# Attention and channel mix on one core: q and k transposed in fp32 as loaded, cast to bf16 in the copy out of PSUM

## The chip, the cores and the metric

The kernel runs on one core of one Trainium2 chip. The metric is the time of one execution on the device, in microseconds (us). Ratios come with a 95% interval. The kernel before took 274.27 us (median of 2 runs, 273.6 to 274.94).

Some names. TensorE (PE in the profile) does matrix products and transposes and writes to PSUM. VectorE is DVE, ScalarE is ACT, GpSimd is POOL, and SyncE (SP) issues most DMAs. A *pair* is two heads of one batch: there are 8 batches of 4 pairs, so pairs 0 to 31. Times inside an execution are counted from the start of its span.

## The reference

```python
# q, k, v: (8, 8, 576, 64) fp32; d_model = 512, d_ff = 1024
scores = q @ k.transpose(0, 1, 3, 2) / sqrt(64)          # per head, 576 x 576
scores = where((rel >= 0) & (rel < 128), scores - slope[h] * abs(rel), -1e9)
attn = softmax(scores); x = attn @ v                     # heads side by side: (8, 576, 512)
x_prev = x shifted by one position
xk = mu_k * x + (1 - mu_k) * x_prev;  xr = likewise with mu_r
out = sigmoid(xr @ w_r) * (relu(xk @ w_k) ** 2 @ w_v)
```

The scores need q and k with the head dimension on the partitions, so both are transposed on the chip. The products of the second half are the greater part of TensorE's work.

## The kernel before

For each pair, q and k are loaded in fp32, cast to bf16, transposed by TensorE eight blocks at a time into one PSUM bank, and copied out by ScalarE into `qk_buf`. The listing is shortened: `...` stands for what is left out.

```python
# H = 8, D = 64, G = 4 pairs per batch, NF = 4, NBUF = 4, SM = 512 rows (the other 64 go another way)
p_sa = pool(bufs=2, PSUM)   # scores: 2 banks each
p_tp = pool(bufs=1, PSUM)   # transposes: one bank
p_mm = pool(bufs=3, PSUM)   # matmuls: one bank each; all 8 banks are taken
ldr = cst.tile([128, 2, NBUF, 2, NF * D], FP32, name="ldr")      # q|k, slot, head, 4 rows of 64

def load_qk(it, npair=1, part=None):
    ...
        if part is None:                                         # 1 KB runs
            nc.sync.dma_start(out=dst, in_=hs[:, 0:SM].rearrange("h (p r) d -> p h (r d)", p=128))
    ...
def pool_cast(dst, src):
    nc.gpsimd.tensor_scalar(out=dst, in0=src, scalar1=1.0, scalar2=0.0, op0=ALU.mult, op1=ALU.add)
def vec_cast(dst, src):
    nc.vector.tensor_copy(out=dst, in_=src)

def cast_qk(it, part=None, fq=pool_cast, fk=vec_cast):
    ...                                                          # r0, r1: rows 0 to NF where part is None
    cs = csp.tile([128, 2, NF, 2, D], BF16, tag="cs", name="cs", bufs=4)
    T["cs", it, part] = cs
    for i, f in ((0, fq), (1, fk)):
        f(cs[:, i, 0:r1 - r0].rearrange("p r h d -> p h r d"),   # puts the two heads side by side
          ldr[:, i, it % NBUF].rearrange("p h (r d) -> p h r d", d=D)[:, :, r0:r1])

def transp(it):
    ...
    cs = T.pop(("cs", it, None))
    tp = p_tp.tile([128, 1024], BF16, tag="tp", name="tp")
    for n in range(2 * NF):
        nc.tensor.transpose(tp[:, 128 * n:128 * n + 128],
                            cs[:, n // NF, n % NF].rearrange("p h d -> p (h d)"), ident)
    nc.scalar.copy(out=qk_buf[it % NBUF].rearrange("p t (c r) -> p t c r", r=NF),
                   in_=tp.rearrange("p (t r c) -> p t c r", t=2, r=NF))

def scores(it, pieces, m0):
    ...                                                          # matmuls of qk_buf into sa
    nc.scalar.activation(out=ah, in_=sa[:, :, 0:w], func=AF.Exp, scale=float(scale))
    if not early:                                                # batches 2 to 7: the mask multiply
        nc.vector.tensor_tensor(out=ah, in0=ah, in1=mask[...], op=ALU.mult)

def feed(it, fk=vec_cast):
    cast_qk(it, None, pool_cast, fk)
    cast_v(it)                                                   # GpSimd
    load_qk(it + 4)
    load_v(it + 4)
    ...
```

Batch 0 has its own path and does not change. Batch 1 (pairs 4 to 7) runs while weights and inputs still load. From pair 8 a loop puts work on TensorE pair by pair, with matmuls of the second half (`run_units`) between the steps. In this loop the program fixes the order of TensorE, SyncE and GpSimd; a scheduler orders VectorE and ScalarE.

```python
    for it in range(2 * G, NIT + 2):
        scores_full(it)
        ...                               # bud: how much of the second half goes into this pair
        run_units(bud * .3)
        av(it - 1, 0, NJ)                 # attention times v
        run_units(bud * .3)
        ...                               # in one pair of four, the tails
        transp(it + 2)
        feed(it + 3)
        ...
        run_units(bud * .4)
        outT(it - 1, 0, NJ)               # transposes of the result, also through p_tp
```

The softmax here doesn't subtract the row's maximum and nothing guards it: scores larger than these inputs give would overflow.

## Time and profile before

| | kernel before |
|---|---|
| time, median of 2 | 274.27 us |
| span of the profiled execution | 272.5 us |
| start of pair 8's scores / from pair 8 to pair 31 / rest | 70.8 / 162.5 / 39.2 us |

The three stages are read from the starts of the score matmuls in the trace. The first block is part of the profile's page: busy time by engine, and the chain of work that ended last, by engine.

```profile
## 1 busy us (share of the span) xinstructions
PE 244.9 (90%) x2272; PEld 145.0 (53%) x2304; DVE 211.4 (78%) x428; ACT 179.9 (66%) x293; POOL 74.0 (27%) x121
...
q1 hardware_dynamic: 71040, 37.76, 51.8%
...
PE 54%; DVE 15%; ACT 11%; DMA 8%; SPq 5%; issue 5%; POOL 2%; DVEq 0%; POOLq 0%; ACTq 0%
```

TensorE is busy 90% of the span and holds 54% of the chain, so it bounds most of the kernel, with VectorE (78%) behind it. The line of q1 is the main DMA queue: packets, MB, and the share of the 16 DMA engines' time.

The next block has groups of instructions of the same kernel, with shapes kept apart: line, engine, operation, output from inputs, count, then busy time and the mean in ns, then idle time of the engine just before.

```profile
L235 DVE TENSOR_TENSOR at<-at,mask 128x1024 bf16<-128x1024 bf16 x48 | 44.6, 968 | 0.8 <-ACT at L233 0.8
L187 ACT COPY qk<-tp 128x1024 bf16<-128x1024 bf16 x28 | 28.4, 1016 | 10.9 <-PE tp L184 10.6
L126 POOL TENSOR_SCALAR cs<-ldr 128x512 bf16<-128x512 f32 x34 | 27.7, 815 | 7.7 <-DMA ldr<-in_q_dram 6.7 <-DMA ldr<-in_k_dram 0.4
L184 PE MATMUL tp<-ident,cs 128*128 128x128 bf16 x224 | 17.1, 219 | 0.0
L184 PEld LDWEIGHTS <-cs 128*128 128x128 bf16 x224 | 14.3, 98 | 4.8 <-issue 0.6 <-POOL cs L126 0.2
L130 DVE CAST cs<-ldr 128x512 bf16<-128x512 f32 x22 | 9.8, 443 | 4.4 <-DMA ldr<-in_k_dram 4.4
```

The casts are L126 on GpSimd (34, among them k's where GpSimd casts both) and L130 on VectorE (22). A bf16 transpose is recorded with 219 ns, but the records of consecutive transposes overlap, so this is not the time that one takes up on TensorE. That time is read from the timeline of TensorE (start, length, engine, line, count), here around one pair's transposes:

```profile
151.18 0.61 PE L184 MATMUL tp<-ident,cs 128*128 128x128 bf16 x8
151.62 1.03 PE L341 MATMUL pv<-wv_sb,kk 128*128 128x512 bf16 x4
```

Eight transposes occupy TensorE for 151.62 - 151.18 = 0.44 us, about 55 ns each.

Last, the table of windows over a steady stretch (after the window: busy us of each engine and number of its instructions, granted TensorE clock, share of the DMA engines, GB/s), and the timeline of VectorE in two places, with GpSimd's between them. All are of the kernel before.

```profile
core 0: us, PE busy (x) PEld busy (x) DVE busy (x) ACT busy (x) POOL busy (x), PEclk, DMA share, GB/s
105.00:164.00 59.00, 56.44 (x553) 33.75 (x558) 54.23 (x102) 42.82 (x66) 17.52 (x20) 1.00 0.59 161
```

```profile
112.52 2.12 DVE L235 TENSOR_TENSOR at<-at,mask 128x1024 bf16<-128x1024 bf16 x2
...
112.33 0.76 POOL L126 TENSOR_SCALAR vs<-vdr 128x512 bf16<-128x512 f32 x1 [3.25 <-issue]
113.06 1.04 POOL L126 TENSOR_SCALAR cs<-ldr 128x512 bf16<-128x512 f32 x1
...
229.91 1.28 DVE L235 TENSOR_TENSOR at<-at,mask 128x1024 bf16<-128x1024 bf16 x2
```

TensorE is busy 56.4 of 59 us and VectorE 54.2. Two mask multiplies take 2.12 us while GpSimd casts beside them, and 1.28 us where GpSimd has nothing left to do.

### The profile page before, as it was taken

How to read it: one execution, taken by the hardware profiler on the slowest of the kernel's cores; microseconds unless marked ns; L12 is line 12 of the kernel's file. 1: busy time of each engine (PE TensorE's matmuls, PEld its weight loads, DVE VectorE, ACT ScalarE, POOL GpSimd, SP SyncE). 2: the span in 40 equal slices, each digit the busy share in tenths (PEclk: the TensorE clock that was granted, in tenths of full speed). 3: DMA queues.
4: the chain of work that ended last, by engine and by line, in shares of the span. 5: the costliest groups of instructions: out<-in, count | busy, mean ns of one | idle time of the engine just before them, and what ended most of it. 6: DMA issues, size and time to landing. Idle time of an engine off the chain costs nothing.

```text
span 272.5 us, 6003 instructions
## 1 busy us (share of the span) xinstructions
PE 244.9 (90%) x2272; PEld 145.0 (53%) x2304; DVE 211.4 (78%) x428; ACT 179.9 (66%) x293; POOL 74.0 (27%) x121
## 2 busy tenths in 40 slices
PE   4589899857999899999999999999999999999994
PEld 1245665525555565545555755555565755455461
DVE  2268973367878999998988899989888888976342
ACT  5468688832795776876686677866685868635350
POOL 5383066513042225222320225222422100000000
PEclk9999999977999999999999999999999999999999
DMA  6999999998593691791686551972501211022122
GB/s 164 226 206 196 241 246 283 247 295 196 160 282 85 177 265 45 191 243 50 195 207 161 154 161 58 232 196 91 177 2 38 81 38 41 0 81 77 38 79 77
DMA packets 73229, 40.77 MB, mean 150 GB/s; under 512 B 48112, under 2 KB 68080, under 8 KB 73200
## 3 DMA queue, kind: packets, MB, share of 16 engines
q1 hardware_dynamic: 71040, 37.76, 51.8%
q0 software_dynamic: 2160, 2.63, 5.8%
q8 instruction: 18, 0.29, 0.5%
q14 instruction: 11, 0.09, 0.1%
HBM read 33.56 MB, written 9.44 MB: 158 GB/s over the span
## 4 chain that ended last, share of the span: by engine, by line
PE 54%; DVE 15%; ACT 11%; DMA 8%; SPq 5%; issue 5%; POOL 2%; DVEq 0%; POOLq 0%; ACTq 0%
PE pv L341 17%; PE ps L312 14%; PE pr L327 8%; PE sa L262 5%; DMA ldr<-in_k_dram 4%; DVE at L235 4%; ACT at L233 4%; ACT xt L289 3%; PE tp L184 3%; DVE xk L300 2%; DMA vdr<-in_v_dram 2%; ACT rl L316 2%; PE sa L230 2%; DVE xr L300 2%; DMA tq<-in_k_dram 2%
## 5 line engine op out<-in xcount | busy, mean ns | idle before, releaser
L312 PE MATMUL ps<-xk,wk_sb 128*128 128x256 bf16 (+2 forms) x413 | 70.7, 313 | 3.9 <-ACT rl L316 1.5
L341 PE MATMUL pv<-wv_sb,kk 128*128 128x512 bf16 x271 | 68.8, 382 | 1.8 <-issue 0.6
L233 ACT ACTIVATE at<-sa 128x1024 bf16<-128x1024 f32 (+1 forms) x68 | 63.7, 983 | 9.3 <-PE sa L230 9.1
L316 ACT ACTIVATE rl<-ps 128x256 bf16<-128x256 f32 (+2 forms) x104 | 47.8, 478 | 22.1 <-PE ps L312 14.3
L126 POOL TENSOR_SCALAR vs<-vdr 128x512 bf16<-128x512 f32 (+1 forms) x36 | 24.6, 686 | 127.8 <-issue 89.6
L312 PEld LDWEIGHTS <-wk_sb 128*128 128x128 bf16 x416 | 38.6, 97 | 25.3 <-issue 6.1
L235 DVE TENSOR_TENSOR at<-at,mask 128x1024 bf16<-128x1024 bf16 x48 | 44.6, 968 | 0.8 <-ACT at L233 0.8
L318 DVE TENSOR_TENSOR kk<-rl 128x256 bf16<-128x256 bf16 (+2 forms) x104 | 35.6, 362 | 10.8 <-ACT rl L316 8.6
L341 PEld LDWEIGHTS <-kk 128*128 128x128 bf16 x288 | 26.1, 98 | 27.8 <-DVE kk L318 2.0
L332 ACT ACTIVATE rs<-pr 128x512 bf16<-128x512 f32 x36 | 21.7, 606 | 24.2 <-PE pr L327 24.2
L347 DVE SCALAR_TENSOR_TENSOR ot<-rs,pv 128x512 f32<-128x512 bf16 x36 | 24.3, 674 | 16.8 <-PE pv L341 16.3
L327 PE MATMUL pr<-wr_sb,xr 128*128 128x512 bf16 x132 | 35.7, 379 | 0.7
L187 ACT COPY qk<-tp 128x1024 bf16<-128x1024 bf16 x28 | 28.4, 1016 | 10.9 <-PE tp L184 10.6
L126 POOL TENSOR_SCALAR cs<-ldr 128x512 bf16<-128x512 f32 (+1 forms) x38 | 29.5, 777 | 7.7 <-DMA ldr<-in_q_dram 6.7
L262 PEld LDWEIGHTS <-at 128*128 128x128 bf16 x576 | 23.8, 102 | 11.9 <-issue 7.6
L300 DVE SCALAR_TENSOR_TENSOR xk<-dl,muk_sb,xt 128x576 bf16<-128x576 bf16 (+2 forms) x36 | 27.1, 753 | 1.2
L300 DVE SCALAR_TENSOR_TENSOR xr<-dl,mur_sb,xt 128x576 bf16<-128x576 bf16 (+2 forms) x36 | 27.3, 759 | 0.0
L298 DVE TENSOR_TENSOR dl<-xt 128x576 bf16<-128x576 bf16 (+2 forms) x36 | 15.8, 440 | 9.6 <-ACT xt L289 9.3
L270 DVE TENSOR_TENSOR xu<-sa,rc 128x640 bf16<-128x640 f32 x28 | 22.7, 814 | 0.3
L262 PE MATMUL sa<-vs,at 128*128 128x65 bf16 x448 | 19.7, 196 | 2.3 <-ACT at L233 1.6
L230 PE MATMUL sa<-qk 64*128 64x256 bf16 (+1 forms) x264 | 21.2, 268 | 0.6 <-ACT qk L200 0.2
L130 DVE CAST cs<-ldr 128x512 bf16<-128x512 f32 (+1 forms) x30 | 12.4, 414 | 11.9 <-DMA ldr<-in_k_dram 11.9
(56 smaller groups left out, 217.3 us busy)
## 6 DMA issues: line engine op xcount, KB each, us to landing
out_dram<-ot SPq DMA_DIRECT2D x36, 256.0 KB, 2.1
ldr<-in_q_dram SPq DMA_DIRECT2D x29, 256.0 KB, 4.2
ldr<-in_k_dram SPq DMA_DIRECT2D x29, 256.0 KB, 4.5
vdr<-in_v_dram SPq DMA_DIRECT2D x56, 128.0 KB, 3.9
vdr<-in_v_dram SPq DMA_DIRECT2D x4, 256.0 KB, 5.6
tq<-in_q_dram SPq DMA_DIRECT2D x8, 128.0 KB, 4.8
tq<-in_k_dram SPq DMA_DIRECT2D x8, 128.0 KB, 4.9
tv<-in_v_dram SPq DMA_DIRECT2D x8, 128.0 KB, 4.9
```

Source lines behind the costliest of these rows:

```text
L126: nc.gpsimd.tensor_scalar(out=dst, in0=src, scalar1=1.0, scalar2=0.0, op0=ALU.mult, op1=ALU.add)
L187: nc.scalar.copy(out=qk_buf[it % NBUF].rearrange("p t (c r) -> p t c r", r=NF), in_=tp.rearrange("p (t r c) -> p t c r", t=2, r=NF))
L230: nc.tensor.matmul(sa[:, hl, c0:c0 + n], lhsT=kk_, rhs=qq_, start=not early, stop=True, skip_group_check=True)
L233: nc.scalar.activation(out=ah, in_=sa[:, :, 0:w], func=AF.Exp, scale=float(scale))
L235: nc.vector.tensor_tensor(out=ah, in0=ah, in1=mask[:, 2 * g:2 * g + 2, m0:m0 + w], op=ALU.mult)
L262: nc.tensor.matmul(a5[:, hl, t - t0], lhsT=at[:, lo:lo + 128], rhs=vs[:, u, hl, :] if u < NF else tvb[:, 2 * g + hl], start=(u == us[0]), ...
L300: nc.vector.scalar_tensor_tensor(out=dst[:, g, S * e + c0:S * e + c1], in0=dl[:, 0:c1 - c0], scalar=mu[:, g:g + 1], in1=xp, op0=ALU.mult, ...
L312: nc.tensor.matmul(ps[:, 0:n], lhsT=wk_sb[:, po, 128 * fo:128 * fo + 128], rhs=xk[:, po, c0:c1], start=(po == 0), stop=(po == NPO - 1))
L316: nc.scalar.activation(out=rl[:, 0:n], in_=ps[:, 0:n], func=AF.Relu, scale=RELU_SCALE)
L318: nc.vector.tensor_tensor(out=kk[:, fo, 0:n], in0=rl[:, 0:n], in1=rl[:, 0:n], op=ALU.mult)
L327: nc.tensor.matmul(pr, lhsT=xr[:, po, 128 * c:128 * c + 128], rhs=wr_sb[:, po], start=(po == 0), stop=(po == NPO - 1))
L341: nc.tensor.matmul(pv, lhsT=kk[:, fo, o:o + 128], rhs=wv_sb[:, fo], start=(fo == 0), stop=(fo == NFO - 1))
```

## The change

The intent is to take the casts of q and k away. From batch 1 on, q and k are loaded with the two heads side by side (runs of 256 B in place of 1 KB), transposed in fp32 straight from the loaded tile, and become bf16 when ScalarE copies them out of PSUM. The one-bank tile of 1024 bf16 columns has room for 512 fp32 columns, four blocks, so q and k are transposed and copied apart, through the same single bank. Why the runs are short: a transpose here reads one stretch of 128 adjacent columns, and these must be two heads of 64.

```diff
+    lds = ldr.rearrange("p i s h c -> p i s (h c)").rearrange(
+        "p i s (r h d) -> p i s r h d", h=2, d=D)
@@ load_qk
+        if b > 0:
+            for i, src in enumerate((q, k)):
+                for hl in range(2):
+                    nc.sync.dma_start(
+                        out=lds[:, i, s0, :, hl],
+                        in_=src[b, 2 * g + hl, 0:SM].rearrange("(p r) d -> p r d", p=128))
+            return
@@ transp
-        cs = T.pop(("cs", it, None))
-        tp = p_tp.tile([128, 1024], BF16, tag="tp", name="tp")
-        for n in range(2 * NF):
-            nc.tensor.transpose(...cs..., ident)
-        nc.scalar.copy(...)                                   # 128 x 1024
+        for i in which:                                       # (0, 1), or one of them
+            tp = p_tp.tile([128, 512], FP32, tag="tp", name="tp")
+            for r in range(NF):
+                nc.tensor.transpose(
+                    tp[:, 128 * r:128 * r + 128],
+                    lds[:, i, it % NBUF, r].rearrange("p h d -> p (h d)"), identf)
+            nc.scalar.copy(
+                out=qk_buf[it % NBUF][:, i].rearrange("p (c r) -> p c r", r=NF),
+                in_=tp.rearrange("p (r c) -> p c r", r=NF))
@@ feed
-        cast_qk(it, None, pool_cast, fk)
         cast_v(it)
-        load_qk(it + 4)
+        load_qk(it + 3)
@@ the loop from pair 8
-        run_units(bud * .3)
+        run_units(bud * .15)
         ...
-        transp(it + 2)
+        transp(it + 2, (0,))
+        run_units(bud * .15)
+        transp(it + 2, (1,))
         feed(it + 3)
... (an fp32 identity, and the other calls of feed without their cast argument, cut)
```

In batch 1, `transp` still does q and k one right after the other. The shorter load depth has a side effect: pair 7 is loaded twice, once at the start and once by the first `feed`.

More of the change, by code (lines that the diff above doesn't have):

```diff
@@ L176, in transp_tail, with transp @@
         nc.vector.tensor_copy(out=tt_buf[b % 2][:, :, 0], in_=t4[:, :, 1])
-    def transp(it):
+    def transp(it, which=(0, 1)):
         if not 0 <= it < NIT:
             return
-        cs = T.pop(("cs", it, None))
-        tp = p_tp.tile([128, 1024], BF16, tag="tp", name="tp")
-        for n in range(2 * NF):
-            nc.tensor.transpose(
-                tp[:, 128 * n:128 * n + 128],
-                cs[:, n // NF, n % NF].rearrange("p h d -> p (h d)"), ident)
-        nc.scalar.copy(
-            out=qk_buf[it % NBUF].rearrange("p t (c r) -> p t c r", r=NF),
-            in_=tp.rearrange("p (t r c) -> p t c r", t=2, r=NF))
+        for i in which:
[7 more added lines that the diff above has]
+                in_=tp.rearrange("p (r c) -> p c r", r=NF))
     def transp_part(it, part):
@@ L353 @@
     ident = cst.tile([128, 128], BF16, name="ident")
+    identf = cst.tile([128, 128], FP32, name="identf")
     mask = cst.tile([128, H, 768], BF16, name="mask")
@@ L439 @@
     make_identity(nc, ident)
+    nc.vector.tensor_copy(out=identf, in_=ident)
     make_dist()
@@ L506 @@
     outT(*span(2 * G - 2))
-    nc.gpsimd.tensor_copy(out=ldr[:, :, 0, 0, 0:1], in_=wr_sb[:, 0:2, 0:1])
+    nc.gpsimd.tensor_copy(out=lds[:, :, 0, 0, 0, 0:1], in_=wr_sb[:, 0:2, 0:1])
     load_qk(G)
@@ L520, in first1, with feed @@
             make_mask(range(fo, fo + 1))
-    def feed(it, fk=vec_cast):
-        cast_qk(it, None, pool_cast, fk)
+    def feed(it):
         cast_v(it)
-        load_qk(it + 4)
+        load_qk(it + 3)
         load_v(it + 4)
@@ L542 @@
     run_units(1800)
-    feed(G, pool_cast)
+    feed(G)
     cast_tail(1)
@@ L546 @@
     transp(G)
-    feed(G + 1, pool_cast)
+    feed(G + 1)
     transp_tail(1)
@@ L562 @@
             av(it - 1, 0, NJ)
-        feed(it + 2, pool_cast)
+        feed(it + 2)
         run_units(bud * .5)
```

## The prediction

> **What bounds it now.** TensorE, with VectorE just behind. Chain of waits: 54% TensorE, 15% VectorE, 11% ScalarE, 8% DMA. In the steady stretch (105 to 164 us, 8 head pairs, 7.38 us each) the table of windows has TensorE about 95% busy, VectorE 92%, ScalarE 73%, DMA 51 to 65%. By the starts of matmuls in the trace, TensorE's own rates (216 ns per 512 columns, 56 ns per bf16 transpose) make 54 of those 59 us: about 0.6 us per pair is slack.
>
> **Removed (28 pairs, batches 1 to 7).** A q cast on GpSimd (1.05 us when steady) and a k cast, 0.41 us on VectorE (22 pairs). Side gain: the mask multiply takes 1.06 us while GpSimd casts, 0.64 us at 224 to 237 us, when GpSimd is idle. The Trainium skill (SBUF — State Buffer, Who interferes with whom) says that a two-input VectorE instruction and a GpSimd read share a port pair; these durations agree. I expect 0.4 us per pair back. VectorE falls from 6.8 to about 6.0 us per pair and stops being a limit; its waits for k loads (11.9 us, 4.4 of them on casts that go) vanish or move to TensorE.
>
> **Added.**
> - Eight fp32 transposes per pair for eight bf16 ones. The trace has no fp32 matmul. The Trainium skill (TensorE: Matmul & The Clock Gate; Terms, and the weight-path modes) says transpose mode makes fp32 4x faster (one pass, I take it), but fast weight load is not for fp32. No separate weight loads stand in the new instruction order, so loads are less hidden: an estimate of 105 to 165 ns each from the page's weight load (128/1.2 = 107 ns) alone, or plus the trace's 56 ns. That is +0.4 to +0.9 us per pair on the limiting engine; in four passes, +1.5 us or more.
> - Two 128x512 copies out of PSUM for one 128x1024: 2 x 0.60 for 1.01 us on ScalarE, which has room.
> - One single-bank buffer takes q, k and attention transposes in turn; k's wait for q's copy. In batch 1 they follow directly: about 0.8 us of TensorE wait in 7 pairs; later, with a block or two of matmuls between, 0.1 to 0.3 us.
> - 256 B packets took 19 ns, 1 KB ones 54, so +0.7 us on every DMA engine per pair: DMA share about 65%, no limit. But from 27 to 55 us DMA is saturated, more issues share the queue, and pair 7 is loaded twice: 2 to 4 us, partly hidden.
>
> **Sum.** 24 steady pairs: +0.6 (transposes) +0.2 (buffer) -0.35 (slack freed by the lighter VectorE) = +0.45 us each, +11 us. Batch 1 and start: +3 us. Predicted 287 us, range 270 to 307. Faster by over 2%: 0.10; within 2%: 0.25; slower by over 2%: 0.65.
>
> **Right or wrong in the profile.**
> - Transposes of ldr start 105 to 165 ns apart (56 before).
> - Mask multiply's mean 0.97 to about 0.75 us; VectorE share 78% to under 68%; GpSimd 74 to about 45 us.
> - New TensorE waits on the qk copy (a few us, most at 40 to 70 us).
> - Main DMA queue's share 52% to about 60%; packets 73 to about 118 thousand.
> - Steady period 7.6 to 8.1 us per pair; TensorE's share of the chain up.
>
> **What would make it wrong.** fp32 transposes as quick as bf16 (then 270 to 276 us, the VectorE gain shows) or in four passes (over 315 us). Late loads through the busier queue stalling TensorE. More slack freed than I count: TensorE's floor before is 6.8 us per pair.

## The result, and the profile after

| | before | after |
|---|---|---|
| time, median of 2 runs | 274.27 us | 285.38 us (285.34 to 285.41) |
| ratio | | 1.0382 [1.0337, 1.0427] |
| span of the profiled execution | 272.5 us | 283.5 us |
| to pair 8 / pair 8 to 31 / rest | 70.8 / 162.5 / 39.2 us | 72.8 / 171.3 / 39.4 us |

Ratios are not quite the ratios of the medians quoted (here 285.38 / 274.27 = 1.0405). By the ratio the kernel became 3.8% slower. The stages say where: 2.0 us before pair 8, 8.9 us from pair 8 to pair 31 (23 intervals, so 0.38 us each), 0.3 us after.

The page and the groups of the changed kernel, in the order in which those of before were shown (shapes kept apart in the groups again):

```profile
## 1 busy us (share of the span) xinstructions
PE 251.9 (89%) x2272; PEld 154.5 (54%) x2304; DVE 199.1 (70%) x407; ACT 184.5 (65%) x321; POOL 48.2 (17%) x87
...
q1 hardware_dynamic: 117056, 38.29, 55.0%
...
PE 65%; ACT 15%; DVE 12%; SPq 3%; issue 3%; DMA 3%; ACTq 0%; DVEq 0%
```

```profile
L244 DVE TENSOR_TENSOR at<-at,mask 128x1024 bf16<-128x1024 bf16 x48 | 40.0, 872 | 0.8 <-ACT at L242 0.8
L193 PE MATMUL tp<-identf,ldr 128*128 128x128 f32 x224 | 35.2, 280 | 8.5 <-ACT qk L196 8.4
L196 ACT CAST qk<-tp 128x512 bf16<-128x512 f32 x56 | 32.8, 585 | 23.2 <-PE tp L193 22.9
L193 PEld LDWEIGHTS tp<-identf,ldr 128*128 128x128 f32 x224 | 24.8, 140 | 20.8 <-ACT qk L196 17.3 <-issue 0.8
```

VectorE's share fell from 78 to 70% and GpSimd's work from 74 to 48 us, as meant. TensorE's share of the chain rose from 54 to 65%. The transposes now carry a wait of 8.4 us for ScalarE's copy (L196) that did not exist.

The rate of the fp32 transposes, from TensorE's timeline of the changed kernel, around one pair's q and then k:

```profile
156.76 0.60 PE L193 MATMUL tp<-identf,ldr 128*128 128x128 f32 x4
157.20 1.03 PE L350 MATMUL pv<-wv_sb,kk 128*128 128x512 bf16 x4
158.09 0.66 PE L193 MATMUL tp<-identf,ldr 128*128 128x128 f32 x4
158.58 1.03 PE L350 MATMUL pv<-wv_sb,kk 128*128 128x512 bf16 x4
```

Four transposes take 157.20 - 156.76 = 0.44 us for q and 158.58 - 158.09 = 0.49 us for k. In 0.44 us eight bf16 ones were done. Over the whole trace the median from one start to the next is 109 ns, against 56 ns. Over 28 pairs of eight transposes this makes 28 x 8 x (109 - 56) = 11.9 us of TensorE. The median leaves one thing out: from pair 8 to 31 the first of each four takes 131 ns on average to the next start, where bf16 ones take 56 ns at every place. No run separates why an fp32 transpose takes longer, so that cause stays open.

The steady stretch of the changed kernel in the table of windows, and then TensorE's waits up to pair 8 (who waited for whom: us in total, times, longest):

```profile
105.00:164.00 59.00, 57.30 (x524) 35.79 (x532) 47.23 (x86) 41.94 (x69) 9.12 (x11) 1.00 0.64 156
```

```profile
PE tp L193 <- ACT qk L196: 5.8, 6, 1.1
PE to L293 <- DVE xu L279: 1.8, 1, 1.8
PE pv L350 <- issue: 0.5, 3, 0.2
```

In the same 59 us TensorE is busier than before although it gets through fewer instructions (524 against 553), while VectorE has 12 us to spare. Of the 8.4 us of waits for the copy out of the single bank, 5.8 us lie before pair 8. In the steady loop a block of matmuls between q and k usually covers the copy, as the timeline above shows; the other 2.6 us are four waits there.

### The profile page after: what moved, and what is told of

It reads as the page before. It is cut to its first block, busy times and chain, and to the rows that moved or that the text cites. A ratio compares the mean times of both kernels' runs of the same rounds, so it can differ in the third digit from the quotient of the medians.

```text
span 283.5 us, 6072 instructions
## 1 busy us (share of the span) xinstructions
PE 251.9 (89%) x2272; PEld 154.5 (54%) x2304; DVE 199.1 (70%) x407; ACT 184.5 (65%) x321; POOL 48.2 (17%) x87
## 4 chain that ended last, share of the span: by engine, by line
PE 65%; ACT 15%; DVE 12%; SPq 3%; issue 3%; DMA 3%; ACTq 0%; DVEq 0%
PE pv L350 20%; PE ps L321 16%; PE pr L336 9%; PE tp L193 9%; ACT at L242 5%; PE sa L271 5%; ACT rl L325 3%; DVE xk L309 3%; ACT xt L298 3%; DMA ldr<-in_k_dram 3%; PE sa L239 2%; DVE xr L309 2%; ACT qk L196 2%; DVE xu L279 2%; DVE at L244 2%
## 5 line engine op out<-in xcount | busy, mean ns | idle before, releaser
L135 POOL TENSOR_SCALAR vs<-vdr 128x512 bf16<-128x512 f32 (+1 forms) x36 | 25.7, 717 | 172.0 <-PE sa L271 89.7
L196 ACT CAST qk<-tp 128x512 bf16<-128x512 f32 x56 | 32.8, 585 | 23.2 <-PE tp L193 22.9
L327 DVE TENSOR_TENSOR kk<-rl 128x256 bf16<-128x256 bf16 (+2 forms) x104 | 34.2, 342 | 17.9 <-ACT rl L325 15.6
L193 PE MATMUL tp<-identf,ldr 128*128 128x128 f32 x224 | 35.2, 280 | 8.5 <-ACT qk L196 8.4
L244 DVE TENSOR_TENSOR at<-at,mask 128x1024 bf16<-128x1024 bf16 x48 | 40.0, 872 | 0.8 <-ACT at L242 0.8
L350 PEld LDWEIGHTS <-kk 128*128 128x128 bf16 x288 | 26.7, 98 | 24.9 <-DVE kk L327 0.4
L193 PEld LDWEIGHTS tp<-identf,ldr 128*128 128x128 f32 x224 | 24.8, 140 | 20.8 <-ACT qk L196 17.3
L271 PEld LDWEIGHTS <-at 128*128 128x128 bf16 x576 | 22.1, 98 | 12.4 <-issue 6.3
L271 PE MATMUL sa<-vs,at 128*128 128x65 bf16 x448 | 19.0, 193 | 3.0 <-ACT at L242 2.6
L298 ACT COPY xt<-tp 128x576 bf16<-128x576 bf16 x24 | 15.3, 636 | 9.2 <-PE tp L293 9.2
```

The costliest lines, as they stand in the source:

```text
L193: nc.tensor.transpose(tp[:, 128 * r:128 * r + 128], lds[:, i, it % NBUF, r].rearrange("p h d -> p (h d)"), identf)
L196: nc.scalar.copy(out=qk_buf[it % NBUF][:, i].rearrange("p (c r) -> p c r", r=NF), in_=tp.rearrange("p (r c) -> p c r", r=NF))
L244: nc.vector.tensor_tensor(out=ah, in0=ah, in1=mask[:, 2 * g:2 * g + 2, m0:m0 + w], op=ALU.mult)
L271: nc.tensor.matmul(a5[:, hl, t - t0], lhsT=at[:, lo:lo + 128], rhs=vs[:, u, hl, :] if u < NF else tvb[:, 2 * g + hl], start=(u == us[0]), ...
L327: nc.vector.tensor_tensor(out=kk[:, fo, 0:n], in0=rl[:, 0:n], in1=rl[:, 0:n], op=ALU.mult)
L350: nc.tensor.matmul(pv, lhsT=kk[:, fo, o:o + 128], rhs=wv_sb[:, fo], start=(fo == 0), stop=(fo == NFO - 1))
```

## The experiments

My theory: the fp32 transposes' rate is most of the cost, because TensorE is the limit; the single bank costs in batch 1; taking the casts away gives little back because VectorE was not the limit. The rivals: the single bank and the second copy cost it throughout; or the loads in short runs do. Twelve kernels ran. The checks on results do not see q and k well: kernels that use wrong q or k on purpose passed too, so "correct" says little about this part.

| kernel | from | median, us | ratio to before [95%] | to pair 8 | pair 8 to 31 |
|---|---|---|---|---|---|
| before | | 274.27 | 1 | 70.8 | 162.5 |
| after | | 285.38 | 1.0382 [1.0337, 1.0427] | 72.8 | 171.3 |
| a_half | after | 275.6 | 1.0038 [1.0000, 1.0076] | 71.0 | 163.3 |
| a_bank | after | 285.06 | 1.0403 [1.0344, 1.0461] | 70.0 | 173.3 |
| b_split | before | 280.23 | 1.0197 [1.0157, 1.0236] | 75.7 | 163.8 |
| b_nocast | before | 269.13 | 0.9800 [0.9761, 0.9840] | 68.5 | 160.1 |
| b_runs | before | 274.94 | 0.9999 [0.9976, 1.0022] | 68.5 | 166.1 |
| b_noq | before | 271.23 | 0.9866 [0.9833, 0.9900] | 69.1 | 160.7 |
| b_nok | before | 270.54 | 0.9824 [0.9786, 0.9862] | 70.3 | 160.5 |
| a_fix | after | 280.07 | 1.0190 [1.0169, 1.0211] | 67.3 | 171.5 |
| a_nodup | after | 285.9 | 1.0400 [1.0363, 1.0437] | 73.8 | 171.5 |
| a_1krun | after | 285.74 | 1.0390 [1.0364, 1.0416] | 73.6 | 171.5 |
| c_mix | both | 272.99 | 0.9930 [0.9903, 0.9958] | 67.1 | 163.8 |
| c_dmacast | before | 277.16 | 1.0112 [1.0069, 1.0155] | 73.5 | 161.8 |

The last two columns come from one profiled execution each. The rest after pair 31 was 39.2 to 39.6 us in all. The start is less sure than the steady stretch: in the profile of before, TensorE's granted clock was half from 57.8 to 64.6 us, in those of b_split, b_runs, b_nocast, b_noq and b_nok it was half for 3.4 us near the same place, and in those of after, a_half and c_mix not at all there. From pair 8 to 31 the granted clock was 1.00 in all of them. The total times carry this too: of the six runs of b_nok two took 268.2 and 268.3 us at mean clocks of 1.000 and 0.999, three 270.4 to 270.8 us at 0.992 to 0.994, and one 271.75 us at 0.981. The runs of before in the later rounds had 0.975 to 0.992.

### a_half: half of the fp32 transposes

```diff
-            for r in range(NF):
+            for r in range(NF // 2):
                 nc.tensor.transpose(...)
+            t2 = tp[:, 0:256].rearrange("p (r c) -> p c r", r=2)
             nc.scalar.copy(
-                out=qk_buf[it % NBUF][:, i].rearrange("p (c r) -> p c r", r=NF),
-                in_=tp.rearrange("p (r c) -> p c r", r=NF))
+                out=qk_buf[it % NBUF][:, i].rearrange("p (c a r) -> p a c r", a=2, r=2),
+                in_=t2[:, None].to_broadcast([128, 2, 128, 2]))
```

> Changed kernel with only four of the eight fp32 transposes per pair (the copy fills q and k from the two blocks twice; result wrong on purpose). Loads, copies and the single bank stay as in the changed kernel; TensorE's transpose time falls back to about that of eight bf16 ones (4 x 109 = 436 ns against 8 x 56 = 448 ns). Theory 'TensorE rate of fp32 transposes': 28 pairs x 436 ns = 12.2 us less than 285.4, so 272 to 275 us. Rival 'the single bank, the extra copies or the 256 B loads cost it': little falls away, 281 us or more.

Measured: 275.6 us, 9.8 us less than the changed kernel, of the 12.2 us of TensorE taken out. From pair 8 to 31 it saved 171.3 - 163.3 = 8.1 us (by unrounded starts), where the 22 pairs transposed in this stretch had 22 x 4 x 109 ns = 9.6 us fewer. So about four fifths of TensorE's time there turned into kernel time, and the rate of fp32 transposes is the main cost in the steady loop. It is not the whole of it: with half of the transposes gone, and no casts, the kernel is still no faster than before. Part of that is the transposes still: from pair 8 to 31 the 88 transposes of a_half, from each start to the next start on TensorE, took 11.7 us, the 176 of before 9.8 us. Of these 1.9 us, 1.0 is one wait for q's copy and 0.9 the slow first transpose of each group (133 ns).

### b_nocast, b_noq, b_nok: what the casts cost

b_nocast lets the casts of batches 1 to 7 work on 128x4 elements only (one column of each row block, of the first head); the transposes read a fixed tile. In b_noq only q's cast shrinks and in b_nok only k's, with the same fixed tiles. There are two of these tiles (`cfix`, made and cleared in lines cut here), where the kernel before has four `cs` tiles.

```diff
+        if it >= G:
+            T["cs", it, part] = cfix[it % 2]
+            for i, f in ((0, fq), (1, fk)):
+                f(cfix[it % 2][:, i, :, 0, 0:1], ldr[:, i, it % NBUF, 0].rearrange(
+                    "p (r d) -> p r d", d=D)[:, :, 0:1])
+            return
```

> Kernel before with the q and k casts of batches 1 to 7 shrunk to one column of each head (result wrong on purpose; the same waits on the loads, the same transposes from a fixed tile). Gives what taking away the casts is worth by itself. My prediction: 0.35 us per pair in 24 pairs, so -8 us, about 266 us, with the mask multiply's mean near 0.75 us. The steady stretch of the changed kernel (+0.28 us per pair with +0.42 of transposes) rather says 0.15 us per pair: -3 to -5 us, 269 to 271. If the casts were free beside TensorE: no change.

> Kernel before with only q's cast (GpSimd; in batch 1 too) shrunk to a column, k's kept; wrong on purpose. Both casts gone gave -5.6 us. If the gain comes from the mask multiply running without GpSimd beside it: -3 to -5 us. If from VectorE's own k cast: -1 us or less.

> Kernel before with only k's cast shrunk (VectorE 22 times, GpSimd in most of batch 1), q's kept; wrong on purpose. If the gain comes from VectorE's k cast and its waits for k loads: -3 to -5 us. If from the mask multiply and GpSimd: -2 us or less.

Measured: 269.13 us without both casts, 5.6 us less than before in the same rounds. The two profiled executions differ by 2.3 us at pair 8 and by 2.4 us in the 23 intervals after it, so 0.10 us per pair. My prediction counted on 0.35 us. Without q's cast alone it is 1.3% less, without k's alone 1.8%; by my expectations each result names its own cast as the cause, and together they exceed the gain without both.

These two runs do not separate the casts, because the fixed tiles also moved the cast that was kept. With two tiles, a cast must wait until the transposes of two pairs earlier have read its tile. GpSimd in b_nok:

```profile
117.86 0.82 POOL L127 TENSOR_SCALAR vs<-vdr 128x512 bf16<-128x512 f32 x1 [3.80 <-PE sa L273]
119.91 0.72 POOL L127 TENSOR_SCALAR cfix<-ldr 128x512 bf16<-128x512 f32 x1 [1.23 <-DMA ldr<-in_k_dram]
```

In before, q's cast followed v's at once (113.06 after 112.33 us) and ran beside the mask multiply. Here it starts 1.2 us after v's has ended. The profile names a DMA as the releaser, but 16 of the 28 casts of q start at the same distance (within 2 ns) from the end of the seventh of the eight transposes of the pair two earlier. The same wait stands before the small casts of b_nocast; whether it changes the 0.10 us is not shown.

The group of the mask multiply in b_nok, which keeps q's cast, shows what this did:

```profile
L246 DVE TENSOR_TENSOR at<-at,mask 128x1024 bf16<-128x1024 bf16 x48 | 40.0, 871 | 0.8 <-ACT at L244 0.8
```

It fell as far as in the kernels without any cast (872 ns). I sorted the 48 multiplies of each trace by whether a GpSimd instruction ran beside them. In before, 39 overlapped one and took 1033 ns on average, 9 did not and took 685 ns. In after it was 29 (998 ns) and 19 (680 ns). In b_nok it was 28 (1007 ns), one with a short overlap, and 19 (682 ns). In before, q's or k's casts met 25 of the 48; in b_nok the casts of `cfix` met 2, although q's was whole. So a multiply was slow whenever GpSimd worked beside it, and the number of meetings is what changed. The casts of v and of the tails remain in the changed kernel and still meet 29 of 48, which is why I had the side gain too large.

### b_split and a_bank: the single bank

b_split keeps casts and bf16, but transposes and copies q and k apart, as the change does. a_bank takes the changed kernel and gives k's transposes a bank of the matmul pool.

```diff
# b_split, against before
-        for n in range(2 * NF): ...                # one tile, one copy
+        cs = T["cs", it, None]
+        for i in which:
+            tp = p_tp.tile([128, 1024], BF16, tag="tp", name="tp")
+            for r in range(NF):
+                nc.tensor.transpose(tp[:, 128 * r:128 * r + 128],
+                                    cs[:, i, r].rearrange("p h d -> p (h d)"), ident)
+            nc.scalar.copy(out=qk_buf[it % NBUF][:, i].rearrange("p (c r) -> p c r", r=NF),
+                           in_=tp[:, 0:512].rearrange("p (r c) -> p c r", r=NF))
# and transp(it + 2, (0,)) ... transp(it + 2, (1,)) in the loop, as in the change

# a_bank, against after
-            tp = p_tp.tile([128, 512], FP32, tag="tp", name="tp")
+            tp = (p_mm.tile([128, 512], FP32, tag="mm", name="tk") if i else
+                  p_tp.tile([128, 512], FP32, tag="tp", name="tp"))
```

> Kernel before with casts, loads and bf16 transposes kept, but q and k transposed and copied apart, in turn through the single bank, at the places where the changed kernel has them. Theory 'fp32 rate': +1 to +5 us (batch 1 waits, ScalarE +0.2 us per pair), 275 to 279 us. Rival 'single bank and two copies': +8 us or more, over 282 us.

> Changed kernel, but k's transposes go to a bank of the three shared matmul banks, so that they need not wait for q's copy. Theory 'fp32 rate': only batch 1's waits go (5.8 us of TensorE waits on the qk copy between 41 and 73 us), 280 to 284 us, steady period unchanged. Rival 'single bank': over 8 us less, 277 us or under. It could also lose by taking a bank from the matmuls for a copy's length.

b_split lost 5.5 us, just above what I had allowed (1 to 5). In the profiled executions, which lie 6.1 us apart, 4.8 us are before pair 8 and 1.3 us in the 23 intervals after it. TensorE's waits before pair 8 in b_split:

```profile
PE tp L185 <- ACT qk L188: 7.0, 6, 1.3
PE to L285 <- DVE xu L271: 3.5, 2, 1.8
```

So the bank is a cost of batch 1, where q's copy stands right between the two halves, and hardly one of the loop (0.06 us per pair).

a_bank, with these waits gone, reached pair 8 at 70.0 us, 2.8 us sooner than the changed kernel, but needed 1.9 us more from there to pair 31. There TensorE waited 2.4 us for `ot`, the VectorE instruction that frees a matmul bank, and in the changed kernel not at all, so the matmuls' having to share their banks fits. Its total, 285.06 us, is about that of the changed kernel: above my range of 280 to 284, and no support for the rival that expected 277 or less. The waits of TensorE up to pair 8 in a_bank show what came in place of the copy:

```profile
PE tp L194 <- DMA ldr<-in_q_dram: 2.6, 2, 1.7
PE to L294 <- DVE xu L280: 1.8, 1, 1.8
PE tk L194 <- DMA ldr<-in_k_dram: 1.6, 2, 0.9
```

With the bank free, the loads are late.

### b_runs and a_1krun: the short runs

b_runs puts the loads of the change into the kernel before, with casts that read them in order. a_1krun takes the short runs out of the changed kernel: the loads are those of before, and the transposes read 128 adjacent columns that are the wrong ones.

```diff
# b_runs, against before: the load_qk block of the change, and
+        if it >= G:
+            for i, f in ((0, fq), (1, fk)):
+                f(cs[:, i], lds[:, i, it % NBUF])
+            return
# a_1krun, against after
-        if b > 0:
-            for i, src in enumerate((q, k)):
-                for hl in range(2):
-                    nc.sync.dma_start(out=lds[:, i, s0, :, hl], in_=...)
-            return
```

> Kernel before with only the loads of the change: q and k of batches 1 to 7 in 256 B runs, two issues per tensor and pair, the casts reading them in order. Casts, transposes and load depth as before, no double load. Theory: the loads cost only in batch 1, where DMA is saturated: +0.7 us of DMA time per pair, 0 to +3 us in all, 274 to 278 us, nothing after pair 8. Rival 'the loads cost it throughout': +5 us or more, growing from pair to pair.

> Changed kernel with the loads of before (1 KB runs, one issue per tensor and pair); the transposes still read 128 adjacent columns, which are then the wrong ones (result wrong on purpose). All else as in the changed kernel, the double load too. In the steady stretch the parts add to about 2 us less than the changed kernel loses (casts -2.4, split +1.3, fp32 rate +8.1; measured +8.9). If the 256 B loads are that rest: 282 to 284 us, with pairs 8 to 31 shortened by 1.5 to 3.6 us. If loads cost nothing there: 285 us, the stretch unchanged.

b_runs took as long as before (0.9999). Its stages moved, 2.3 us sooner at pair 8 and 3.6 us longer from there to pair 31, but the scheduler had also put VectorE's casts at other places, so I don't ascribe this to the loads. a_1krun settles it for the changed kernel: the order of VectorE and ScalarE is the same as in the changed kernel, the packets fall from 117 to 72 thousand, and the time does not fall (285.74 us; 171.5 against 171.3 us from pair 8 to 31).

```profile
q1 hardware_dynamic: 71584, 38.28, 49.7%
```

The short runs cost 5 points of the DMA queue's share and no time.

### a_fix and a_nodup: repairs of the start

```diff
# a_nodup, against after
-        load_qk(it + 3)
+        if it > G:
+            load_qk(it + 3)
# a_fix: this, and
-            tp = p_tp.tile([128, 512], FP32, tag="tp", name="tp")
+            tp = (p_mm.tile([128, 512], FP32, tag="mm", name="tk")
+                  if i and it < 2 * G + 2 else
+                  p_tp.tile([128, 512], FP32, tag="tp", name="tp"))
```

> Changed kernel with two repairs of the start: k's transposes of batch 1 and the first two pairs of batch 2 go to a bank of the matmuls (no wait for q's copy), and pair 7 is loaded once. With k in a matmul bank throughout, pair 8 began 2.8 us sooner than in the changed kernel, but the steady stretch was about 2 us longer, and 4.2 us of TensorE waits for loads stood in batch 1. Theory: 280 to 283 us, steady stretch as in the changed kernel (+0.38 us per pair on before). If it came to 277 or less, the single bank would be a greater part of the cost than the fp32 rate.

> Changed kernel with only the double load of pair 7 taken out. The repaired start gained 5.3 us with both repairs, the bank alone 0.3 us at the end (2.8 us at pair 8). If the two repairs add in batch 1: 1 to 2.5 us less than the changed kernel, 283 to 284.5 us. If loads hide behind the wait for q's copy: no change, 285 us.

a_fix took 280.07 us, 5.3 us less than the changed kernel, with pair 8 at 67.3 us and the steady stretch unchanged (171.5). TensorE's waits up to 68 us in a_fix are now short:

```profile
PE to L295 <- DVE xu L281: 1.6, 1, 1.6
PE tk L195 <- DMA ldr<-in_k_dram: 0.8, 1, 0.8
PE pv L352 <- issue: 0.5, 3, 0.2
```

Taking the double load out alone did nothing (285.9 us, ratio 1.0400 against 1.0382): the waits for q's copy (5.8 us up to pair 8 there too) hid it. With the bank alone pair 8 began at 70.0 us, with both at 67.3 us. So the two repairs do not add; the second shows only when the first is made.

### c_dmacast: casts by the DMAs

```diff
+        if b > 0:
+            cs = csp.tile([128, 2, NF, 2, D], BF16, tag="cs", name="cs", bufs=4)
+            T["cs", it, None] = cs
+            for i, src in enumerate((q, k)):
+                for hl in range(2):
+                    nc.gpsimd.dma_start(
+                        out=cs[:, i, :, hl],
+                        in_=src[b, 2 * g + hl, 0:SM].rearrange("(p r) d -> p r d", p=128))
+            return
```

(`feed` then has no `cast_qk`, and loads pair it + 3 when it is above 4.)

> Kernel before with q and k of batches 1 to 7 cast to bf16 on their way in, by DMAs of GpSimd's queue, into the tile that the bf16 transposes read; no casts by an engine. The ceiling is the run without casts, 269 us. If GpSimd's issues (0.8 to 0.9 us each in this trace, four per pair) disturb nothing: 269 to 272 us. If they hold the v casts up or slow the mask multiply (GpSimd beside VectorE): 275 us or more.

It took 277.16 us, 1.1% more than before. The steady stretch (161.8 us) was nearly that of before, but pair 8 began at 73.5 us. The profile has one wait of 4.1 us of TensorE for a GpSimd cast of the tails (`ts`), which stands behind these issues in GpSimd's order, and GpSimd's busy time rose to 131.6 us, 84.1 of them issues. The casts are not free this way.

### c_mix: each form where it paid

Pairs 4 to 9 go as in a_fix: fp32, k in a matmul bank, short runs, each loaded once. Pairs 10 to 31 go as before, with casts and bf16 transposes.

```diff
+    X = 2 * G + 2
@@ load_qk
+        if G <= it < X: ...                     # the short runs of the change
@@ transp
+        if it < X: ...                          # fp32, as in a_fix
@@ feed
-        cast_qk(it, None, pool_cast, fk)
+        if it >= X:
+            cast_qk(it, None, pool_cast, fk)
         cast_v(it)
-        load_qk(it + 4)
+        if G < it <= X:
+            load_qk(it + 3)
+        if it >= X:
+            load_qk(it + 4)
```

> The change where it paid, the kernel before where it did not: pairs 4 to 9 (batch 1 and the start of batch 2) in fp32 with k in a matmul bank and 256 B runs, loaded once; pairs 10 to 31 with casts, bf16 transposes and 1 KB runs. With the repaired start the changed kernel reached pair 8 at 67.3 us against 70.8 before; the steady stretch of before took 9 us less than that of the changed kernel. If the parts add: about 3 us under before, 270 to 273 us. If the gain at the start is lost at the seam (casts and loads of pairs 10 to 13 late): 274 to 276 us.

It took 272.99 us, ratio 0.9930 [0.9903, 0.9958]: 0.7% faster than the kernel before and 4.3% than the changed one (272.99 / 285.38, of other rounds). Pair 8 began at 67.1 us, as in a_fix; the steady stretch was 163.8 us, 1.3 us longer than before. What the 0.7% comes from is not shown. The profile of before has 6.8 us at half clock ahead of pair 8 and that of c_mix none there; at most 3.4 us of TensorE's work were lost in it (an estimate: half of 6.8), nearly the 3.7 us gained at pair 8. The six runs of c_mix had mean clocks of 0.993 to 1.000, the eleven of before in these rounds 0.975 to 0.988, so the times do not separate the form from the clock either.

## Why the prediction was right

The time (285.38 for 287 us), the direction and the limit were right. Point by point:

- **TensorE is the limit, and the fp32 transposes load it.** Right. Predicted 105 to 165 ns from start to start, measured 109 ns, the low end. The Trainium skill (TensorE: Matmul & The Clock Gate, Terms) says that the transpose mode is 4x faster for fp32; the trace shows no four-fold cost, but twice that of bf16, and shows a weight load of 140 ns against 98 ns. The term was put at +0.6 us per pair; the rate makes 8 x 53 ns = 0.42 us, and a_half shows 8.1 us over 22 pairs = 0.37 us as kernel time. Mis-sized, 1.6 times too large. The reason given for it, weight loads less hidden, is not tested by any run.
- **The single bank.** Predicted 0.2 us per pair in the loop and 0.8 us in each of 7 pairs before it, with +3 us for the whole start. b_split shows 1.3 us over 23 intervals = 0.06 us in the loop, and 4.8 us before pair 8. The mechanism is the one predicted; the loop's part was three times too large.
- **Slack freed by the lighter VectorE.** Predicted 0.35 us per pair, measured 2.4 us over 23 intervals = 0.10 us in b_nocast. This is the term that was most wrong. VectorE did drop (54.2 to 47.2 us in the steady 59 us), but there was not that much slack behind it. From pair 8 to 31 of before the profile has TensorE idle for 8.3 us; its waits above 150 ns were 3.4 us for VectorE, or 0.15 us per interval, and 2.6 us for ScalarE. In b_nocast the waits for VectorE fell to 1.8 us and those for ScalarE rose to 3.6 us: another engine ended part of the waits in its place. The slack of 0.6 us per pair in the prediction came from matmul rates, not from such waits.
- **The three errors cancelled in part, which is luck.** The terms as measured in the other kernels make 0.37 + 0.06 - 0.10 = 0.33 us per interval, the changed kernel lost 0.38 us, and I had 0.45. In the same eight pairs as the 7.38 us of before, the period came to 7.64 us (7.6 to 8.1 predicted). Over the stretch the measured terms make 8.1 + 1.3 - 2.4 = 7.0 of 8.9 us. Of the missing 1.9 us, up to 0.9 us is the part of the fp32 rate that a_half leaves in; the rest, near 1 us, is not explained. The loads are not it (a_1krun). The scheduler's order of VectorE and ScalarE differs between these kernels, which could be it; I have no run that holds that order fixed.
- **Mask multiply.** Predicted mean 0.75 us, measured 0.872, because v's casts still run beside 29 of 48. The Trainium skill (SBUF — State Buffer, Who interferes with whom) says that a two-input VectorE instruction and a GpSimd read contend; the sorted durations (680 to 685 ns alone, 998 to 1033 ns beside GpSimd) agree. VectorE's share came to 70%, not under 68; GpSimd to 48 us (45 predicted).
- **DMA.** Predicted +0.7 us of each DMA engine per pair and a queue share of 60%; the share came to 55%, the packets to 119 thousand (118 predicted). No limit, as said. The start: +2.0 us measured, +3 predicted. It is a sum of larger things: casts -2.3 us, bank +4.8 us, fp32 rate +1.7 us (after against a_half), and a remainder of -2.2 us that one profile each, with different clocks, can't assign. The 6.8 us at half clock in before alone could be worth up to 3.4 us (half of them, an estimate), so that the start agrees with the +3 is partly luck.

## What to carry to other kernels

Before moving work off an engine, ask whether that engine ends the waits of the one that limits: here a cast that vanished from VectorE and GpSimd gave back 0.10 us per pair, and the transposes that paid for it cost 0.37 us on TensorE. A change can cost differently by stage. Even at the start, where TensorE also waits for loads, the fp32 transposes were not free: a_half, with 6 x 4 x 109 ns = 2.6 us of them less there, began pair 8 1.7 us sooner. A kernel that used them only there, with the bank repaired, took less time than both, but a higher granted clock can be the reason. Two waits in a row hid each other here, so a repair without effect may be good once the wait before it is gone. And a stand-in for work that is taken away, such as the fixed tiles of b_nok, can bring a wait of its own: look at when the work that stays now runs.

## What the Trainium skill lacked or had wrong

- TensorE: Matmul & The Clock Gate, Part 4 (PE-mode transpose), has figures for bf16 only. Measured here: a 128x128 fp32 transpose every 109 ns (record 280 ns, its weight load 140 ns), a bf16 one every 56 ns (record 219 ns, weight load 98 ns). The page gives about 275 ns for bf16 in a kernel, as a duration; what a busy TensorE pays is the distance between starts, a fifth of that.
- The same part says that the full clock doesn't engage for transposes, since they don't count as busy in the same way. In the steady stretch the granted clock was 1.00 and bf16 transposes started 56 ns apart, the page's own figure for a warm 128-column matmul, so transposes among matmuls ran at the full rate. Whether transposes alone would bring the full clock, no run here shows.
- SBUF — State Buffer, Who interferes with whom, says that a VectorE instruction with two SBUF inputs contends with a GpSimd read, but gives no duration for it. Here a 128x1024 bf16 multiply beside GpSimd casts took 998 to 1033 ns on average against 680 to 685 ns alone.
- DMA: Bandwidth & Descriptors warns of transfers under 512 B. On the main queue packets of 256 B took 18 ns of a DMA engine (changed kernel) and 1 KB ones 54 ns (before) on average (14 and 19 bytes per ns), but with the queue at 55% the short runs cost no time at all (285.38 us with them, 285.74 without).
